# Attention in 64-row tiles, and 32-column tiles for the other products, in a fused gated mix of an S4D convolution and segmented attention

## The chip, the cores and the metric

The kernel runs on one core of a Trainium2 chip. The metric is device time in microseconds for one execution. The core has five engines that run on their own and wait for each other by semaphores: PE (matrix products into PSUM), DVE (vector), ACT (scalar functions), POOL (GpSimd) and SP, which issues most of the transfers. PE loads a block of weights and then streams columns past it. The array can be used whole (128 rows x 128 columns), or as tiles of 64 or 32 rows or columns; tiles on different rows or columns can work side by side.

## The reference

Input `x` is 2048 x 448. The result mixes two branches with a gate per row.

```python
x = A_u                                            # (1, 2048, 448)
g = sigmoid((x * gate_w).sum(-1, keepdims=True))
# A: diagonal state space model as a long convolution, N = 256 states
K = 2 * einsum("dn,dnl->dl", C, exp((A * dt)[:, :, None] * pos)).real
y = irfft(rfft(x.T, 2 * L) * rfft(K, 2 * L))[..., :L].T + x * D_skip
# B: 16 heads of 28, four segments of 512, softmax attention and a running memory
for s in range(4):
    p = softmax(qs @ ks.T * scale + mask)           # causal within the segment
    a_dot = p @ vs
    a_mem = (phi(qs) @ M) / (phi(qs) @ z + 1e-6)
    o = g_h * a_mem + (1 - g_h) * a_dot
    M, z = M + phi(ks).T @ vs, z + phi(ks).sum()
b = concat(o) @ wo
return g * y + (1 - g) * b
```

All data is float32.

## The kernel before, in words

The program has two halves. The **first half** builds the convolution kernel `kb` from sines and exponentials, and beside it runs the projections to q, k and v, the memory terms and the first Fourier step of `x`. Tables of numbers (FEED, FILL, UNREAD, VECTOR) say at each slot how many steps of the projections are fed in, how many Fourier steps fill gaps, how many dummy matmuls go ahead of a sum (`turn_over`, UNREAD), and whether copies run on DVE or on ACT. q and k go to DRAM as a high and a low part (`QD`, `KD`), 32 rows per head: 28 of the head and one (row 28) of ones in k, which in q takes the negated maximum of each row.

The **second half** works on 16 units, each of one segment and four heads. Its order is a string of words, PROGRAM, each letter one step, recorded in this order on PE:

- `l` loads q and k of a unit (`load`), `A` computes one block of maxima (`maxima`): a product of q and k for two heads, then a reduction on DVE. After six `A` comes `B`, which transposes the maxima and writes them, high and low, into row 28 of q through a small transfer that POOL issues.
- `W` is one of six steps of `weigh`: for one block and two heads, products of k and q and an exponential on ACT. Three products (high x high, low x high, high x low) give the accuracy. `P` does two `W` of the same block abreast, with four heads on the four 32-row groups.
- `V` multiplies the weights `PT` with the values (four 32-column tiles), `E` is a step of a segment's end (division, memory, output projection `out_mm`), `K` a Fourier step of `kb` (`transform_k`), `C` a step of the convolution (`transform`, `product`, `back`), and `b`, `j`, `z` the last Fourier step (`finish`), `D` a division in the last segment.
- `t` is a filler, a product of a tile of ones (`wz`) that nobody reads.

PSUM has two `ps_m` and three `ps_a` buffers; nearly all steps need a `ps_a` buffer, which ACT or DVE sets free. The loads go to SP's queue in the order in which a scheduler places them among the other transfers; a load waits there until its buffer is free. There are four buffers each for q and k.

A float32 product runs as two passes over its columns, each with its own weight load; q, k and the split parts are of a kind that takes one pass.

## Time and profile before

| | us |
|---|---|
| median of three runs | 835.19 (832.37 to 835.3) |
| the profiled execution | 836.45 |
| its span, first to last instruction | 834.7 |
| PE busy | 727.2 (87%) |
| DVE busy | 569.5 (68%) |
| ACT busy | 555.2 (67%) |
| POOL busy | 239.1 (29%) |

Busy time is the union of an engine's instructions, so it is no rate: matmuls are pipelined, and each one's row also holds the time that it takes to come out of the array. Where the prediction needs the time that a group holds PE, it takes the distance from the group's first start to the next group's first start. In a row, `ps_a<-qu,ku` names the tile written and the tiles read, `32*128` the rows and columns of the array that are used, and `x6` the number of instructions. The first product of the second half (`kb` with `s1k`) starts at 437.8 us.

### The profile page before, as it was taken

What the parts mean: (1) busy time and instruction counts of PE and PEld (TensorE: products, weight loads), DVE (VectorE), ACT (ScalarE), POOL (GpSimd) and SP (SyncE); (2) the same over time, 40 slices, a digit from 0 to 9 for tenths busy, and PEclk for the clock granted to TensorE, in tenths of its full rate; (3) what the DMA queues carried; (4) which work ended last, traced back from release to release, by engine and by line L of the source; (5) the groups of instructions that cost most, each with busy time, mean ns of one, the idle gap of its engine ahead of it and who ended that gap; (6) DMA issues with size and microseconds to landing.
All of it is one profiled execution on the core that took longest, in us unless ns stands there. A gap on an engine that the chain in (4) does not pass through costs nothing.

```text
span 834.7 us, 19015 instructions
## 1 busy us (share of the span) xinstructions
PE 727.2 (87%) x7557; PEld 398.3 (48%) x7582; DVE 569.5 (68%) x1134; ACT 555.2 (67%) x663; POOL 239.1 (29%) x249
## 2 busy tenths in 40 slices
PE   1576998999879999799979899999999899988977
PEld 1353555665546655456644454444444344444433
DVE  7969489857989579886785864544554545666773
ACT  3767789979999899988872266765466544641320
POOL 4404210111001111011110035564545545752210
PEclk9879999999999999999995889999999899999999
DMA  8527775145552455513647877685466565556775
GB/s 206 157 60 241 226 241 175 59 137 181 176 169 66 137 177 178 170 54 135 201 150 295 306 238 219 196 269 172 171 215 215 156 233 175 194 185 253 216 227 150
DMA packets 91987, 153.99 MB, mean 184 GB/s; under 512 B 23106, under 2 KB 60346, under 8 KB 91850
## 3 DMA queue, kind: packets, MB, share of 16 engines
q1 hardware_dynamic: 82826, 141.70, 53.2%
q10 hardware_dynamic: 7424, 9.18, 3.2%
q0 software_dynamic: 1648, 1.89, 0.8%
q8 instruction: 60, 0.98, 0.5%
q14 instruction: 29, 0.24, 0.1%
HBM read 91.74 MB, written 60.63 MB: 183 GB/s over the span
## 4 chain that ended last, share of the span: by engine, by line
PE 45%; DVE 18%; ACT 16%; DMA 9%; issue 7%; POOL 2%; SPq 1%; ACTq 0%; DVEq 0%; POOLq 0%
PE ps_m L1429 19%; PE ps_a L1429 18%; ACT cs L1394 7%; DVE Y L399 4%; DVE jk L1063 4%; PE ps_arg L1429 3%; PE ps_k L1429 3%; DVE X L395 2%; DVE Y L400 2%; ACT L1394 2%; PE ps_m L1432 1%; DMA r<-RD 1%; ACT EX L1394 1%; DMA bt<-BB 1%; DMA ce<-in_c_ce 1%
## 5 line engine op out<-in xcount | busy, mean ns | idle before, releaser
L1063 DVE CUSTOM_DVE_ANT_0 jk<-ps_a,mk 128x512 f32<-128x512 f32 (+3 forms) x256 | 125.1, 489 | 77.7 <-PE ps_a L1429 69.6
L361 POOL TENSOR_TENSOR EX<-EX,cab 128x1024 f32<-128x1024 f32 x28 | 53.5, 1913 | 301.7 <-ACT EX L1394 277.5
L1099 ACT ACTIVATE PT<-ps_a 128x1024 f32<-128x1024 f32 (+1 forms) x96 | 83.0, 880 | 69.6 <-PE ps_a L1429 68.6
L1394 ACT ACTIVATE cs<-ps_arg 128x1024 f32<-128x1024 f32 x111 | 107.4, 1023 | 1.4 <-DVE Y L400 0.8
L1429 PE MATMUL ps_a<-qu,ku 32*128 32x384 f32 (+3 forms) x768 | 78.3, 351 | 5.9 <-DVE mx L1063 5.0
L1429 PE MATMUL ps_m<-xh,w 128*128 128x512 f32 x224 | 81.8, 417 | 1.7 <-DMA w<-WD 1.4
L395 DVE TENSOR_TENSOR X<-EX,cs 128x1024 f32<-128x1024 f32 x56 | 69.2, 1236 | 17.8 <-ACT cs L1394 17.6
L663 POOL TENSOR_TENSOR pr<-us,ks 128x896 f32<-128x896 f32 x32 | 67.1, 2095 | 30.2 <-ACT us L662 30.1
L1110 POOL TENSOR_SCALAR_AFFINE_SELECT PT<-PT 128x256 f32<-128x256 f32 (+1 forms) x96 | 48.2, 507 | 93.3 <-ACT PT L1099 91.7
L1429 PE MATMUL ps_k<-Y,X 128*32 128x64 f32 x3584 | 62.2, 221 | 14.3 <-DVE Y L400 14.0
L1429 PEld LDWEIGHTS ps_k<-Y,X 128*32 128x32 f32 x3584 | 52.9, 110 | 39.1 <-DVE Y L400 27.0
L399 DVE TENSOR_TENSOR Y<-EY,cs 128x1024 f32<-128x1024 f32 x56 | 70.0, 1251 | 0.0
L1429 PEld LDWEIGHTS ps_a<-qu,ku 32*128 32x128 f32 x768 | 55.3, 193 | 20.2 <-DVE mx L1063 9.7
L1394 ACT ACTIVATE EY<-ps_arg 128x1024 f32<-128x1024 f32 x52 | 53.0, 1034 | 17.8 <-PE ps_arg L1429 16.4
L1394 ACT ACTIVATE cs<-cs 128x1024 f32<-128x1024 f32 x56 | 59.3, 1059 | 1.8
L401 DVE SCALAR_TENSOR_TENSOR Y<-EY,cs 128x512 f32<-128x512 f32 x56 | 40.9, 732 | 27.9 <-ACT cs L1394 25.8
L1429 PEld LDWEIGHTS ps_m<-xh,w 128*128 128x128 f32 x224 | 42.0, 187 | 21.9 <-issue 7.9
L1429 PE MATMUL ps_a<-ku,qu 32*128 32x512 f32 (+3 forms) x256 | 47.4, 404 | 4.5 <-DVE mx L1063 1.7
L1429 PE MATMUL ps_arg<-ct,lh 64*128 64x512 bf16 x224 | 45.5, 380 | 6.0 <-ACT cs L1394 4.3
L1429 PE MATMUL ps_m<-xl,w 128*128 128x512 f32 x128 | 50.2, 393 | 0.0
L1429 PEld LDWEIGHTS <-lh 64*128 64x128 bf16 x392 | 22.9, 95 | 55.2 <-issue 41.7
L1429 PEld LDWEIGHTS ps_a<-ku,qu 32*128 32x128 f32 x256 | 23.1, 195 | 48.2 <-issue 21.8
(215 smaller groups left out, 1429.4 us busy)
## 6 DMA issues: line engine op xcount, KB each, us to landing
w<-WD SPq DMA_DIRECT2D x32, 448.0 KB, 4.5
qu<-QD SPq DMA_DIRECT2D x16, 512.0 KB, 4.0
ku<-KD SPq DMA_DIRECT2D x16, 512.0 KB, 5.1
GU<-gs SPq DMA_DIRECT2D x32, 224.0 KB, 2.4
GK<-gs SPq DMA_DIRECT2D x8, 896.0 KB, 4.7
gk<-GK SPq DMA_DIRECT2D x32, 224.0 KB, 3.8
gu<-GU SPq DMA_DIRECT2D x32, 224.0 KB, 2.5
BB<-bs ACTq DMA_DIRECT2D x16, 448.0 KB, 4.5
```

Of the source, the lines that this page charges most:

```text
L361: nc.gpsimd.tensor_tensor(o, o, cab, ALU.mult)
L395: v.tensor_tensor(X, ex, t[:, :, 0], ALU.mult)
L399: v.tensor_tensor(Y[:, :, :, :32], lo, y[:, :, :, ::-1], ALU.mult)
L400: v.tensor_tensor(Y[:, 0, :, 32:], ey[:, :, 32:], y[:, 0], ALU.mult)
L401: v.scalar_tensor_tensor(Y[:, 1, :, 32:], ey[:, :, 32:], -1.0, y[:, 1], ALU.mult, ALU.mult)
L663: nc.gpsimd.tensor_tensor(pr[c], us, ks.pop(c), ALU.mult)
L1063: v.tensor_tensor_reduce(junk[:, :n], pt[:, x, o : o + n], k.mk[:, SEG - n :], 1.0, -3e38, ALU.add, ALU.max, mx[:, 3 - t, h : h + 1],)
L1099: nc.scalar.activation(PT[:, 2 * hp : 2 * hp + 2, 512 * b : 512 * b + n], pt[:, :, :n], AF.Exp, scale=SCALE)
L1110: nc.gpsimd.affine_select(sl, sl, pat, ALU.is_ge, 0.0, base=0, channel_multiplier=-1)
L1394: x = op(*args, **kw)
L1429: tc.keep_in_program_order(nc.tensor.matmul(*args, **kw))
L1432: tc.keep_in_program_order(nc.tensor.transpose(*args))
```

## The change

- **Attention in tiles of 64 rows.** q of a head stands with its high part on 32 rows and its low part on the next 32; two heads on 64 rows each fill the array, and the other two heads of the unit stand behind them in the tile. k stands twice, once for each part, as a high and a low tile. One product over 64 rows now adds q's high and low part times k's high part; a second one does the same with k's low part. So `weigh` takes two products where it took three, and `maxima` still one. The two heads of a step use the rows 0 to 63 and 64 to 127; which pair it is no longer decides on the rows. The words for two steps abreast (`P`) are gone.
- **Loads.** A unit's load is eight transfers of 32 rows (four of q, four of k) instead of two; unit 0 is loaded by POOL's queue. The negated maxima go out in four transfers instead of one. There are three buffers each for q and k instead of four; the first two `PT` tiles and the first tile of values get their place ahead of them.
- **Tiles of 32 columns.** `mm4` cuts a product into four of 32 columns of weights side by side: back transform, last Fourier step, output projection, division, and the filler `t`. A new filler `T` is a pair of products in 64-row tiles. `k` is a `K` whose copies both run on ACT.
- **Tables and words.** FEED, FILL, UNREAD, VECTOR and PROGRAM are written anew. In the first half the gate's weights come by POOL's queue, and the second copy of 64 columns of `xin` is made by POOL from the first instead of by a transfer.

```diff
@@ out_mm; back, last, divide alike
-            k.mm(
+            k.mm4(
...
@@ load
-        for t, T, src in (("q", Q, k.QD), ("k", K, k.KD)):
-            T[i] = ap.tile([128, 2, SEG], F32R, tag=t, name=t + "u", bufs=4)
-            x = k.dma(T[i].bitcast(F32), src[s, hg])
-        if i < 3:
+        Q[i] = ap.tile([128, 2, SEG], F32R, tag="q", name="qu", bufs=3)
+        K[i] = ap.tile([128, 2, 2, SEG], F32R, tag="k", name="ku", bufs=3)
+        qd = k.QD[s, hg].rearrange("(p j e) b q -> j b e p q", p=2, j=2)
+        kd = k.KD[s, hg].rearrange("(p j e) b q -> j e p b q", p=2, j=2)
+        for j in range(2):
+            for b in range(2):
+                r = slice(64 * j + 32 * b, 64 * j + 32 * b + 32)
+                queue = k.dma if i else k.pdma
+                queue(Q[i][r].bitcast(F32), qd[j, b])
+                x = queue(K[i][r].bitcast(F32), kd[j])
+        if 0 < i < 3:
@@ maxima
-                    h = 2 * hp + x
-                    r = slice(32 * h, 32 * h + 32)
+                    r = slice(64 * x, 64 * x + 64)
                     k.mm(
-                        pt[:, x, o : o + n], q[r, 0, 128 * qt : 128 * qt + 128], kk[r, 0, :n],
-                        start=True, stop=True, tile_position=(32 * h, 0),
+                        pt[:, x, o : o + n], q[r, hp, 128 * qt : 128 * qt + 128], kk[r, hp, 0, :n],
+                        start=True, stop=True, tile_position=(64 * x, 0),
                     )
...
-        k.pdma(q.rearrange("(j e) i q -> e j i q", e=32)[28].bitcast(F32), mn.bitcast(F32))
+        for b in range(2):
+            for j in range(2):
+                r = 64 * j + 32 * b + 28
+                k.pdma(q[r : r + 1].bitcast(F32), mn[2 * j : 2 * j + 2, b].bitcast(F32))
@@ weigh
-                for a, (x, y) in enumerate(((0, 0), (1, 0), (0, 1))):
-                    for (_, hp), pt in zip(now, pts):
-                        for z in range(2):
-                            h = 2 * hp + z
-                            r = slice(32 * h, 32 * h + 32)
-                            k.mm(
-                                pt[:, z, o : o + n], kk[r, x, 128 * kt : 128 * kt + 128], q[r, y, 128 * kt :],
-                                start=(a == 0), stop=(a == 2), tile_position=(32 * h, 0),
-                            )
+                for a in range(2):
+                    for z in range(2):
+                        r = slice(64 * z, 64 * z + 64)
+                        k.mm(
+                            pt[:, z, o : o + n], kk[r, hp, a, 128 * kt : 128 * kt + 128], q[r, hp, 128 * kt :],
+                            start=(a == 0), stop=(a == 1), tile_position=(64 * z, 0),
+                        )
@@ turn_over
-            k.mm(pt, wz[:, :128], wz, start=True, stop=True)
+            k.mm4(pt, wz[:, :128], wz, start=True, stop=True)
+    def turn_halves(n):
+        pt = k.ps("a")
+        for _ in range(n):
+            for h in range(2):
+                r = slice(64 * h, 64 * h + 64)
+                k.mm(pt[:, h], wz[r, :128], wz[r], start=True, stop=True, tile_position=(64 * h, 0))
...
@@ gated_mix
+    def mm4(out, w, x, **kw):
+        first = kw.pop("first", 0)
+        for j in range(0, w.shape[-1], 32):
+            mm(out[j : j + 32], w[:, j : j + 32], x, tile_position=(0, first + j), **kw)
@@ PROGRAM, one row of it
-ECAPVBCAWCtAWCtttAWCCtttAWCWV
+WCCVWVBCAWtECCtAWEEEtttCAWAtttttAWWVttttCAl
```

The tables' other rows tell a reader nothing by themselves; the order in which PE's instructions stand says more. Here are places in the two built programs, where a row reads line, operation, tile written and tiles read, shape and count. In the middle of the second half, PE before (`ku,qu` is a maxima pair, `qu,ku` a weigh step, `wo,pvs` the output projection, `gk,cf` a transform of the convolution):

```order
L1429 MATMUL ps_a<-ku,qu 128x256 x2
L1429 MATMUL ps_a<-qu,ku 128x256 x6
L1429 MATMUL ps_m<-wo,pvs 128x448 x4
L1429 MATMUL ps_a<-gk,cf 128x448 x2
L1429 MATMUL ps_a<-ku,qu 128x512 x2
L1429 MATMUL ps_a<-qu,ku 128x512 x6
```

and PE after, in a stretch of the same stage (`gu,cf` is the other transform, `r_7650,sel` a step of the division):

```order
L1453 MATMUL ps_a<-qu,ku 128x512 x4
L1453 MATMUL ps_a<-gu,cf 128x448 x2
L1453 MATMUL ps_m<-r_7650,sel 128x512
L1453 MATMUL ps_a<-ku,qu 128x256 x2
L1453 MATMUL ps_a<-gk,cf 128x448 x2
L1453 MATMUL ps_a<-ku,qu 128x256 x2
```

A weigh step has four products for two heads where it had six, and the maxima stand beside transforms, which now have the same tile shape, as often as beside a weigh step. At the start of the second half, PE before:

```order
L1429 MATMUL ps_k<-Y,X 32x64 x32
L1429 MATMUL ps_a<-kb,s1k 128x448 x8
L1429 MATMUL ps_a<-ku,qu 128x512 x2
L1429 MATMUL ps_a<-kb,s1k 128x448 x8
L1429 MATMUL ps_a<-ku,qu 128x512 x2
```

and PE after:

```order
L1453 MATMUL ps_k<-Y,X 32x64 x32
L1453 MATMUL ps_a<-kb,s1k 128x448 x16
L1453 MATMUL ps_a<-ku,qu 128x512 x2
L1453 MATMUL ps_a<-kb,s1k 128x448 x8
L1453 MATMUL ps_a<-ku,qu 128x512 x2
```

Two steps of `K` now stand ahead of the first maxima instead of one. The load of unit 0 stands on POOL behind the last scaling of the first half (`EX`), where it was on SP behind the last stores of the first half; the loads of units 1 and 2 stay on SP.

106 lines of the change are left out of this document (58 added, 48 removed), and 64 rows, old and new, of tables (FEED, FILL, UNREAD, VECTOR).

## The prediction

> **What bounds the kernel now.** I cut the execution into stages first: the end of the first half (the first matmul on `kb`, 437.8 us), the first product of weights and values (488.9), and the twelfth (729.3). The view of busy time by stretches gives, after the two times, PE, weight loads, DVE, ACT, POOL, the granted clock, the DMA share and GB/s.
>
> ```profile
> 0.00:437.80 437.80, 363.50 (x5102) 228.73 (x5106) 346.47 (x484) 368.28 (x435) 82.97 (x65) 0.96 0.50 157
> 437.80:488.90 51.10, 46.18 (x253) 24.18 (x256) 33.15 (x105) 13.21 (x16) 3.86 (x8) 0.68 0.83 306
> 488.90:729.30 240.40, 228.83 (x1632) 104.26 (x1645) 124.98 (x419) 144.73 (x175) 125.00 (x138) 0.98 0.63 198
> 729.30:834.70 105.40, 88.70 (x575) 41.12 (x577) 64.93 (x130) 28.98 (x38) 27.23 (x40) 0.96 0.66 208
> ```
>
> The middle stage (240.4 us) is bound by PE: 228.8 us busy at a clock of 0.98, while ACT has 144.7, DVE 125.0 and POOL 125.0. The opening of the second half (51.1 us) has PE busy for 46.2 us, but at a clock of 0.68 and with the DMA engines at 0.83. The tail (105.4) is a mixture of PE and waits. In the first half ACT, PE and DVE all stand near 80%.
>
> Then I read the order of matmuls in the middle for what PE does with that time; each row is start, duration, line, and the tile's rows*columns.
>
> ```profile
> 504.69 0.49 PE L1429 MATMUL ps_a<-ku,qu 32*128 32x512 f32 x2
> 504.80 0.96 PE L1429 MATMUL ps_a<-qu,ku 32*128 32x512 f32 x6
> 505.70 0.39 PE L1429 MATMUL ps_m<-wz 128*128 128x512 bf16 x1
> ...
> 529.42 1.02 PE L1429 MATMUL ps_a<-gu,cf 64*128 64x448 f32 x4
> 530.28 0.92 PE L1429 MATMUL ps_a<-gk,cf 64*128 64x448 f32 x4
> 531.13 0.50 PE L1429 MATMUL ps_a<-ku,qu 32*128 32x384 f32 x4
> 531.52 1.07 PE L1429 MATMUL ps_a<-qu,ku 32*128 32x384 f32 x12
> 532.53 1.02 PE L1429 MATMUL ps_a<-gu,cf 64*128 64x448 f32 x4
> ...
> 537.13 0.39 PE L1429 MATMUL ps_a<-ku,qu 32*128 32x256 f32 x2
> 537.14 0.62 PE L1429 MATMUL ps_a<-qu,ku 32*128 32x256 f32 x6
> 537.68 1.02 PE L1429 MATMUL ps_a<-gk,cf 64*128 64x448 f32 x4
> 538.64 0.82 PE L1429 MATMUL ps_m<-wz 128*128 128x512 bf16 x3
> 539.39 0.38 PE L1429 MATMUL ps_a<-ku,qu 32*128 32x256 f32 x2
> ```
>
> Three things are to be seen. First, **a change of tile shape costs time at both ends**. The group at 537.68 (shape entered and left by a change) holds PE until 538.64, 0.96 us. The one at 529.42 (entered by a change, followed by its own shape) takes 0.86, and the one at 530.28 (entered from its own shape, left by a change) 0.85. So the work itself is 0.86+0.85-0.96 = 0.75 us, entering costs 0.11 and leaving 0.10: 0.2 us for a visit. Second, **a maxima pair runs beside the first product of a weigh step**: 504.69 and 504.80, 537.13 and 537.14. They stand on different 32-row groups, so four tiles work at once. Third, three fillers take 0.75 us (538.64 to 539.39) with one change in it: about 0.22 us each for 512 columns.
>
> **The change part by part.** Sums are made against the profiled execution (836.45 us, span 834.7); the median of the runs shown is 835.19, 1.3 us lower.
>
> *Three products to two.* Now a step of maxima and weigh takes 1.01 us for the first block (504.69 to 505.70), 1.40 for the second (531.13 to 532.53) and 0.55 for the third (537.13 to 537.68): 2.96 us for one head pair, 16 x 2 = 32 of them. After it, maxima and weigh use the same two 64-row tiles, so nothing runs beside anything: three slots in a row (one maxima, two weigh). A slot of 512 columns is taken at the filler's 0.22 us, 384 columns at 0.17, and 128 or 256 columns at 0.12, since a weight load, which took 0.11 where it stood open at the entry, does not get shorter. First block: 0.11 + 3 x 0.22 + 0.10 = 0.87; second: 0.11 + 3 x (0.17 + 0.12) + 0.10 = 1.08; third: 0.11 + 3 x 0.12 + 0.10 = 0.57. Sum 2.52, or 0.44 less; 32 times that is 14 us, some 10 us of it in the middle stage (11 of 16 units). I note how little that is: the third product goes, but so does the four-tile overlap that hid the maxima. The nine double steps (the word P, two weigh steps abreast in three slots) now need four slots: 0.22 us each, five of them in the middle, 1 us back.
>
> *Fewer shapes.* Weigh, maxima and both transforms of the convolution are now all 64*128; values, back transform, output projection and fillers all 128*32. Counted in the built order of the second half without fillers, the changes of shape fall from 201 to 143. With the fillers they are 280 in both, because there are more fillers, and in the middle stage 209 against 184: 25 fewer x 0.2 = 5 us. A product cut into four column tiles streams the same columns side by side, so I cost the cutting itself at nothing. What supports this is the product of weights and values, which already runs so; two rows of the order in time, then two groups with their busy time and mean ns.
>
> ```profile
> 509.52 2.36 PE L1429 MATMUL ps_m<-PT,V 128*32 128x512 f32 x32
> 511.82 0.60 PE L1432 MATMUL ps_m<-ident,mx 128*4 128x128 f32 x4
> L1429 PE MATMUL ps_m<-wo,pvs 128*128 128x448 f32 x96 | 40.6, 569 | 1.0 <-DVE pvs L1187 0.7 <-PE ps_m L1429 0.3
> L1429 PE MATMUL ps_m<-wz 128*128 128x512 bf16 x119 | 37.6, 399 | 5.4 <-ACT tb L1203 1.7 <-DVE pvs L1187 1.5 <-issue 1.2
> ```
>
> Four heads of 512+384+256+128 = 1280 columns took 2.30 us, 1.8 ns per column of four tiles. The output projection holds 40.6 us in 96 records of half a product, which is 0.42 us for 448 columns, or 1.9 ns per column for its two halves. The two are equal, so the bounds of this edit are -2 and +2 us.
>
> [...]
>
> *More fillers.* The words hold 196 `t` and 17 `T` for 141 `t`: 72 more x 0.22 = 16 us if none lay in a wait. By place: 45 more before the first values product, where PE waits anyway, 9 more each in the middle and in the tail: 2 us each.
>
> *Loads and the maxima rows.* K now comes twice, 1 MB for 0.5 per unit, 8 MB in all, and a unit's load is eight issues instead of two; the maxima rows go by four POOL issues instead of one.
>
> ```profile
> 488.78 0.33 SPq L1445 DMA_DIRECT2D qu<-QD x1
> 489.15 0.43 SPq L1445 DMA_DIRECT2D ku<-KD x1
> qu<-QD SPq DMA_DIRECT2D x16, 512.0 KB, 4.0
> ku<-KD SPq DMA_DIRECT2D x16, 512.0 KB, 5.1
> L1075 POOL DMA_DIRECT2D qu<-mn x16 | 9.6, 602 | 56.0 <-DVE mn L1074 54.5 <-DVE mx L1063 1.5
> ```
>
> The SP issues go from 0.8 us to 4 x (0.33 + 0.43) = 3.0 us a unit, the POOL ones from 0.6 to 2.4. On SP the loads of the convolution stand behind them, on POOL the masks of `PT` and the products `pr`. POOL has 115 us idle in the middle, against 11 x 1.8 = 20 us added, and a unit's rows are issued three or more weigh steps ahead of their first use. I take nothing, with +8 us as the upper bound (a third rival has the case where it fails).
>
> *The opening.* Here the first load is late; two rows of the chain of waits, two of POOL, and the busy time of the first 20 us:
>
> ```profile
> 436.97 5.04 DMA ku<-KD
> 442.15 3.39 PE ps_a L1429 x16
> 411.64 1.91 POOL L361 TENSOR_TENSOR EX<-EX,cab 128x1024 f32<-128x1024 f32 x1 [20.70 <-ACT EX L1394]
> 415.54 1.91 POOL L361 TENSOR_TENSOR EX<-EX,cab 128x1024 f32<-128x1024 f32 x1 [1.99 <-ACT EX L1394]
> 440.00:460.00 20.00, 17.68 (x90) 9.42 (x83) 11.89 (x32) 4.58 (x5) 0.00 (x0) 0.57 0.78 300
> ```
>
> After the change unit 0 is loaded on POOL, behind its last scaling (over at 417.5), so it can be there before 437; that takes the 5 us wait off the chain. But the K transforms that follow ran at half clock (0.57 here), 3.39 us for sixteen matmuls, and go on until the clock comes back. I count some 66 fillers in this stage, 66 x 0.22 = 15 us of PE, put where PE waits. The work done by the same mark is more (nine weigh steps instead of seven). Between -8 (wait gone, clock up) and +6 (1.5 MB more at 306 GB/s is 5 us, where the DMA share is already 0.83) I take 0.
>
> *First half.* The new tables hold the same sum of steps (249) and move three copies net from ACT to DVE; 70 more dummy matmuls at 0.07 us each make at most 5 us of PE.
>
> ```profile
> 428.82 1.07 PE L1429 MATMUL ps_k<-ct,one 128*128 128x128 bf16 x16
> ```
>
> The sixteen small loads that go are replaced by sixteen POOL copies behind the large ones. I take 0, between -5 and +5.
>
> **Sum.** Middle: -10 (products) +1 (P) -5 (shapes) +2 (fillers) = -12. Tail: four units' share of the products -3.5, P +1, fillers +2, six more changes of shape +1: 0. Opening 0, first half 0. 836.45 - 12 = 824.5, and less the 1.3: about 823; I say 824.
>
> **The rivals.**
>
> 1. *The opening too gets shorter.* If the clock is up from 437 on, the K transforms halve. Half clock costs the opening 51.1 x (1-0.68) = 16 us of PE at most, of which I allow 10, and the 5 us wait goes: 824 - 14 = 810. For it: the first load moves to an idle queue. Against: the words again begin with two K transforms, and the DMA share is 0.83.
>
> 2. *Nothing is won.* The freed slots are taken by fillers and new waits: DVE's reductions and the three `ps_a` buffers set the pace, as DVE waits for `ps_a` and PE for DVE in turn. Then the middle stays at 240: 835. For it: as many changes of shape as before, and 72 more fillers. Against: DVE and ACT are at 52 and 60% in the middle.
>
> 3. *Loads come late (slower).* There are three buffers instead of four, and in the words the load of unit 8, for one, stands six words ahead of that unit's first maxima (load, W, V, B, C, E, A): 0.7 + 2.3 + 0.6 + 0.95 us by the rows above and about 1 for E, some 5.8 us of PE, where before a dozen words and more lay between. Landing then takes 5.1 us plus the 2.2 us that the last issue is later. If SP does not run ahead of PE, PE stands about 1.5 us at each of 13 units, 20 us: 844. It decides from 0.9 us per unit on, where 12 us are used up. Against: SP's issues wait only for buffers, and the third buffer is free one to four weigh steps earlier.
>
> 4. *Loads of weights on the same row group stand open.* All 384 slots of attention are now on the same two groups. If no load could pass under a matmul on its own group, the 288 slots that I counted as covered would take 0.11 us and then their columns (0.22, 0.16, 0.05, 0.11) instead of 0.22, 0.17, 0.12, 0.12: 0.085 us more on average, 24 us in all, so 848. Against it are the rows above: the step at 504.69 took 1.01 us with three weigh products on one group; with each load open it would be 0.11 + 3 x (0.11 + 0.22) + 0.10 = 1.20. [...]
>
> **How the numbers follow.** Forecast 0.50; rival 1 0.20, rival 2 0.16, rival 3 0.10, rival 4 0.04. A measurement of this kernel tells about 0.5% (4 us) from no change. The forecast's own range is 815 to 832, nearly all of it faster; with rival 1 and a tenth of rival 2 that makes 0.71 faster. Same: most of rival 2 and a little of the forecast, 0.16. Slower: rivals 3 and 4, 0.13. For 8 in 10 the range must hold the forecast, most of rival 1 and rival 2: 805 to 838.
>
> **What would show it.** Right: the stretch between the first and the twelfth values product is near 228 us with PE over 95% busy; a step of the first block takes about 0.9 us and of the second 1.1; the maxima no longer start beside a weigh product; a transform followed by a weigh step shows no 0.1 us gap. Wrong: PE idle ended by loads of `ku` (rival 3), equal spacing of 0.33 us between weigh slots (rival 4), a middle stage as long as now with more fillers in it (rival 2). Rival 1 shows as a clock near 1 in the first 20 us of the second half. A first half that moves by more than 5 us would make the sum wrong whatever attention does.

## The result, and the profile after

The changed kernel takes 871.64 us (median of 4 runs, 869.44 to 877.92), beside 834.07 us for the kernel before on the same chip: a ratio of 1.046, 95% interval 1.0405 to 1.0523. It is slower by 4.6%, where 1.3% faster was forecast. Some executions of one and the same kernel took over 1.5% longer than its fastest (836.73 us beside 823.21 in `b_first_p0`); they count in the medians below and not in the ratios, which are each taken against the kernel before on the same chip. The profiled execution took 877.92 us with a span of 876.2. Cut at the same marks (first matmul on `kb`, first and twelfth product of weights and values), the view of busy time by stretches gives for the changed kernel, columns as in the prediction:

```profile
0.00:431.40 431.40, 369.60 (x5174) 234.32 (x5174) 350.57 (x487) 367.20 (x432) 93.73 (x92) 0.97 0.52 162
431.40:493.70 62.30, 56.34 (x495) 25.48 (x495) 32.45 (x106) 15.72 (x19) 7.46 (x15) 0.86 0.80 245
493.70:762.70 269.00, 240.84 (x2062) 109.30 (x2060) 127.48 (x409) 139.82 (x173) 139.32 (x169) 0.93 0.74 198
762.70:876.20 113.50, 97.62 (x946) 40.12 (x944) 64.77 (x134) 29.41 (x39) 31.64 (x50) 0.92 0.71 208
```

Against 437.8, 51.1, 240.4 and 105.4 us before: the first half is 6 us shorter, the opening 11 us longer, the middle 29 us longer and the tail 8 us longer. In the middle PE is busy for 12 us more and waits for 17 us more (269.0 - 240.84 against 240.4 - 228.83).

What it waits for stands in the page's groups and DMA issues and in the first row of the waits view (us in total, times, longest):

```profile
L1453 PE MATMUL ps_a<-ku,qu 64*128 64x512 f32 (+3 forms) x256 | 54.1, 433 | 26.1 <-DMA ku<-KD 16.9
L1453 PE MATMUL ps_a<-qu,ku 64*128 64x256 f32 (+3 forms) x512 | 68.7, 370 | 7.8 <-DVE mx L1077 4.3
...
ku<-KD SPq DMA_DIRECT2D x60, 256.0 KB, 5.5
...
gk<-GK SPq DMA_DIRECT2D x32, 224.0 KB, 5.4
gu<-GU SPq DMA_DIRECT2D x32, 224.0 KB, 6.9
PE ps_a L1453 <- DMA ku<-KD: 16.9, 8, 3.7
```

and, for the two loads of spectra, on the page of the kernel before:

```profile
gk<-GK SPq DMA_DIRECT2D x32, 224.0 KB, 3.8
gu<-GU SPq DMA_DIRECT2D x32, 224.0 KB, 2.5
```

The first maxima of a unit now stand still for the unit's own keys; and the spectra `gk` and `gu`, whose loads stand behind the units' loads on SP, land 5.4 and 6.9 us after their issue, where the kernel before had 3.8 and 2.5. The chain of waits, cut to the middle stage, says the same in shares of that stage:

```profile
by line: PE ps_a L1453 30.6%; PE ps_m L1453 19.6%; DMA ku<-KD 13.9%; SPq L1479 5.8%; DMA xt<-in_A_u 5.0%; DVE jk L1077 4.0%; issue 3.2%; DMA TB<-xt 3.0%; DVE xt L1226 2.3%; DMA dn<-pvs 2.3%; POOL pr L663 1.6%; POOL qu L1092 1.3%; POOL xt L1
```

13.9% of 268 us is 37 us in which the chain runs through a load of `ku`, and 16 us more (5.8%) through SP's issues. One unit in order of time, SP's queue and then PE:

```profile
535.71 0.32 SPq L1479 DMA_DIRECT2D qu<-QD  x1
536.08 0.70 SPq L1479 DMA_DIRECT2D ku<-KD  x1
...
539.27 0.43 SPq L1479 DMA_DIRECT2D ku<-KD  x1
539.80 0.37 SPq L1479 DMA_DIRECT2D gk<-GK  x1
```

```profile
535.17 1.71 PE L1453 MATMUL ps_a<-qu,ku 64*128 64x256 f32 x12
...
543.18 0.54 PE L1453 MATMUL ps_a<-ku,qu 64*128 64x512 f32 x1
545.91 0.47 PE L1453 MATMUL ps_a<-ku,qu 64*128 64x512 f32 x1 [2.20 <-DMA ku<-KD]
```

The load of unit 5 needs the buffer of unit 2. Unit 2's last weigh step is among the twelve matmuls from 535.17, the first of the eight issues comes at 535.71, the last at 539.27, and the chain gives that one 6.50 us to land. The first matmul of unit 5's maxima is at 543.18, and the second stands 2.20 us for the last piece. In the kernel before, every unit's load but that of unit 0 was issued 15 us or more ahead of its first maxima: unit 4's at 488.78 and 489.15, its first maxima at 504.69 (rows in the prediction).

### The profile page after: what moved, and what is told of

The parts are those of the page before. It is cut to its first block, busy times and chain, and to the rows that moved or that the text cites. A ratio compares the mean times of both kernels' runs of the same rounds, so it can differ in the third digit from the quotient of the medians.

```text
span 876.2 us, 21521 instructions
## 1 busy us (share of the span) xinstructions
PE 764.4 (87%) x8673; PEld 409.2 (47%) x8673; DVE 575.3 (66%) x1136; ACT 552.2 (63%) x661; POOL 272.2 (31%) x324
## 4 chain that ended last, share of the span: by engine, by line
PE 42%; DMA 16%; DVE 14%; ACT 11%; issue 9%; SPq 5%; POOL 2%; ACTq 0%; DVEq 0%; POOLq 0%
PE ps_m L1453 20%; PE ps_a L1453 12%; DMA ku<-KD 6%; PE ps_arg L1453 4%; ACT cs L1418 4%; PE ps_k L1453 4%; SPq L1479 3%; DVE Y L399 3%; DVE X L395 2%; DVE jk L1077 2%; DVE Y L400 2%; PE ps_m L1456 2%; DMA xt<-in_A_u 2%; DMA WD<-wsp 1%; ACT L1418 1%
## 5 line engine op out<-in xcount | busy, mean ns | idle before, releaser
L395 DVE TENSOR_TENSOR X<-EX,cs 128x1024 f32<-128x1024 f32 x56 | 70.2, 1254 | 13.9 <-ACT cs L1418 13.8
L1453 PE MATMUL ps_a<-ku,qu 64*128 64x512 f32 (+3 forms) x256 | 54.1, 433 | 26.1 <-DMA ku<-KD 16.9
L1453 PE MATMUL ps_a<-qu,ku 64*128 64x256 f32 (+3 forms) x512 | 68.7, 370 | 7.8 <-DVE mx L1077 4.3
L1453 PE MATMUL ps_m<-wz 128*32 128x512 bf16 x784 | 66.0, 415 | 0.2
L1453 PEld LDWEIGHTS ps_a<-qu,ku 64*128 64x128 f32 x512 | 46.8, 200 | 33.2 <-issue 13.4
L401 DVE SCALAR_TENSOR_TENSOR Y<-EY,cs 128x512 f32<-128x512 f32 x56 | 42.7, 764 | 26.6 <-ACT cs L1418 24.0
L1453 PEld LDWEIGHTS ps_a<-ku,qu 64*128 64x128 f32 x256 | 25.2, 198 | 63.6 <-issue 41.2
L1453 PEld LDWEIGHTS ps_m<-xh,w 128*128 128x128 f32 x224 | 42.0, 187 | 21.3 <-issue 9.0
L1092 POOL DMA_DIRECT2D qu<-mn x64 | 32.6, 515 | 58.6 <-ACT mn L1087 57.9
L1088 DVE SCALAR_TENSOR_TENSOR mn<-ps_m,mn 4x512 fp32r<-4x512 f32 x16 | 10.8, 678 | 60.4 <-ACT mn L1087 60.2
```

Of the source, the lines that this page charges most:

```text
L395: v.tensor_tensor(X, ex, t[:, :, 0], ALU.mult)
L401: v.scalar_tensor_tensor(Y[:, 1, :, 32:], ey[:, :, 32:], -1.0, y[:, 1], ALU.mult, ALU.mult)
L1092: k.pdma(q[r : r + 1].bitcast(F32), mn[2 * j : 2 * j + 2, b].bitcast(F32))
L1453: tc.keep_in_program_order(nc.tensor.matmul(*args, **kw))
```

## The loads

**Without the loads.** The first question is what all late loading costs together. This kernel leaves out the loads of units 3 to 15 (13 x 1.5 MB); these units compute on the tiles of units 0 to 2, so its output is of other data.

```diff
     def load(i):
         if i >= 16:
             return
+        if i >= 3:
+            Q[i], K[i] = first3[i % 3]
+            return
...
+        first3[i] = Q[i], K[i]
```

> The changed kernel in which units 3 to 15 load no q and k: they work on the tiles of units 0 to 2 again (13 of 16 loads left out, so the output is of other data). Theory 1 (late loads: with three buffers a load can be issued only when the weigh steps of the unit three before are over, and that unit's first maxima is then 5 to 10 us away): the waits on ku go, 872 falls to 835 to 848. Theory 2 (the 72 added fillers and their changes of shape hold PE): 862 to 872, since the fillers are all still there. Theory 3 (cutting products into 32-column tiles costs PE time): 862 to 872.

Measured 835.01 us (828.87 to 837.92), ratio 0.998 [0.994, 1.002]: 37 us less than the changed kernel, and just the time of the kernel before. Its middle stage and its tail in the view by stretches:

```profile
491.80:733.40 241.60, 230.77 (x2062) 104.89 (x2060) 128.19 (x409) 139.82 (x173) 139.61 (x169) 0.96 0.49 149
733.40:833.50 100.10, 88.68 (x946) 37.38 (x944) 65.07 (x134) 29.21 (x39) 32.12 (x50) 1.00 0.66 209
```

So 27 of the middle's 29 us belong to the loads (269.0 against 241.6), and 13 of the tail (113.5 against 100.1), more than it had grown. It also says that what is left of the change, with its loads free, wins nothing as a whole.

This trace also shows how much time a load has, since nothing stands for loads in it. From the last weigh step of the unit three before, which frees the buffer, to a unit's first maxima it has 6.9 to 19.5 us, with a median of 10.4. The eight issues and the landing of the last piece took 3.6 + 6.5, some 10 us, in the rows above, so the units with 7 to 9 us come too late. In the kernel before, with four buffers, the same distance (from the unit four before) is 16.0 to 33.3 us. Waits of PE that end with a load of `ku` add up to 16.9 us only; how the rest of the 37 us divides between the loads queued behind and the doubled bytes was not separated.

**A buffer less, alone.** The kernel before with three `q` and `k` buffers and nothing else changed:

```diff
-            T[i] = ap.tile([128, 2, SEG], F32R, tag=t, name=t + "u", bufs=4)
+            T[i] = ap.tile([128, 2, SEG], F32R, tag=t, name=t + "u", bufs=3)
```

> The kernel before with three buffers for q and k instead of four; nothing else is changed. Theory 1: the same words with the same 32-row products lose as the changed kernel with these words did: 900 to 960. If the loss belongs to the doubled k and the eight issues: 835 to 845.

Measured 917.45 us, ratio 1.102 [1.094, 1.110]: 82 us for the fourth buffer. In its waits view:

```profile
PE ps_a L1429 <- DMA ku<-KD: 60.4, 14, 7.5
```

A unit is seven `W` (six weigh steps and the masks). Counted in these words, each `l` from unit 3 on stands four to six `W` ahead of the sixth of the unit three before. With four buffers that costs nothing that shows (827.19 us with the loads of units 3 to 15 and 826.17 without them, both behind the new first half, below); with three, a load has to wait until that unit is through, and the chain of waits from 490 to 790 us runs for 62 us (20.7%) through loads of `ku`. How late the transfers behind it on SP's queue come was not shown.

**The old words with the new loads.** The changed kernel with the words of the kernel before, each `P` written as `WW`:

```diff
 PROGRAM = """
-KKlAkAtttltAAtAtKAttKKKttttttttttttVTTTTTKAttBttAttGtTTTCTAAtttA
...
-tCttWWVBCCAWtAtAWttVCWtAWtAtWCCtAClw
...
+KlAKAAlKAKKAAtAKKBAKtVGCttAtttAtttAttt
...
+lAVWWtCABCAWCtAWCtttWACWtttACWwAV
...
```

> The changed kernel with the words of the kernel before (each P written as WW). The loads stand about a unit earlier in these words, but there are still three buffers. Theory 1: a load placed early holds SP's queue until its buffer is free, and what stands behind it is late too: 865 to 890. Theory 4 (the new words are the fault, not the buffers): 830 to 850.

Measured 971.25 us, ratio 1.163 [1.154, 1.171], far above both theories. So the new words are not what makes the loads late. They soften it: each of their `l` stands one or two `W` behind the sixth of the unit whose buffer it takes. The loads' price is 147 us under the old words (971.25 against 824.63 without them, a kernel further below) and 37 under the new ones (871.64 against 835.01). In the trace of the old words without loads the time from release to first maxima has a median of 1.3 us, where the new words left 10.4.

**The fourth buffer given back.** Queries and the high part of the keys get four buffers, and the low part has tiles of its own (three, loaded later by a word `m`, since only the weigh steps read them). To make room, `ks` has 2 buffers for 3, `bs` 1 for 2, `bt` 4 for 5. Old words.

```diff
-        Q[i] = ap.tile([128, 2, SEG], F32R, tag="q", name="qu", bufs=3)
-        K[i] = ap.tile([128, 2, 2, SEG], F32R, tag="k", name="ku", bufs=3)
+        Q[i] = ap.tile([128, 2, SEG], F32R, tag="q", name="qu", bufs=4)
+        K[i] = [ap.tile([128, 2, SEG], F32R, tag="k", name="ku", bufs=4), None]
...
+        K[i][1] = ap.tile([128, 2, SEG], F32R, tag="kl", name="kl", bufs=3)
```

> The changed kernel with k's high and low part in tiles of their own: four buffers for q and k high (loaded together), three for k low, which is loaded later by a step of its own. Room for it comes from ks (3 to 2), bs (2 to 1) and bt (5 to 4). The words are those of the kernel before, P written as WW. With three buffers these words took 971 us. Theory 1 (the missing fourth buffer is the cause of the loss): the loads are issued a unit ahead again, no waits on ku, 815 to 835. If it is the eight issues or the 8 MB more: 850 or more.

Measured 862.22 us, ratio 1.034 [1.026, 1.042]. The buffers, with the later load of the low part, are worth 109 us under these words (971 to 862). Together with the 82 us of the run before, the missing buffer is the cause of most of the loss under the old words. But 28 us above the kernel before remain, where theory 1 had none: this is the outcome that was set down for the eight issues or the 8 MB more. The remainder is not pure, since a unit's load is now twelve issues and ScalarE waits 17.8 us at its copies into `ks`, which has one buffer less; its parts were not separated.

**Eight issues, alone.** The kernel before with each load cut into four of 32 rows; same bytes, buffers and words.

```diff
-            x = k.dma(T[i].bitcast(F32), src[s, hg])
+            for r in range(0, 128, 32):
+                x = k.dma(T[i][r : r + 32].bitcast(F32), src[s, hg, r : r + 32])
```

> The kernel before with each of a unit's two loads cut into four of 32 rows, so eight issues on SP as in the changed kernel, with the same bytes, buffers and words. Theory 10a (the number of issues alone delays nothing, since the loads are issued 15 to 30 us ahead): 832 to 838. Theory 10b (eight issues fill SP's queue so that the convolution's loads behind them come late): 845 or more.

Measured 841.67 us (840.77 to 844.03), ratio 1.011 [1.006, 1.015]: 8 us, between the two theories. In its one profile the opening is 2.3 us and the middle 3.2 us longer than before. The same ten microseconds of the opening, while the units 0 to 2 are loaded, of the kernel before and then of this one:

```profile
450.00:460.00 10.00, 9.25 (x50) 4.76 (x45) 5.61 (x18) 2.75 (x3) 0.00 (x0) 0.63 0.77 310
```

```profile
450.00:460.00 10.00, 9.68 (x54) 4.69 (x50) 6.47 (x22) 2.40 (x3) 0.00 (x0) 0.66 1.04 305
```

The rate is the same (310 and 305 GB/s), but the DMA engines are busy for 0.77 of the time in the one and for all of it in the other: with the loads in pieces of 32 rows, the traffic of this stretch occupies them a third longer per byte (403 against 293 GB/s per full share). Why the pieces occupy the engines longer was not shown: no run here separates their 32 rows from their smaller size, or the 8 us from the time of six more issues a unit.

## The two products and the words

**Two products against three, loads out of the way.** Two kernels with the same words (the old ones) and the same new first half, both without the loads of units 3 to 15: one with the new tiles and two products, one with the old tiles and three. Both compute on other data, as above. The first is the kernel without loads above with the old words put in as before; in the second the same lines go into `load` of the kernel with the new first half (shown near the end):

```diff
     def load(i):
...
+        if i >= 3:
+            Q[i], K[i] = first3[i % 3]
+            return
         for t, T, src in (("q", Q, k.QD), ("k", K, k.KD)):
...
```

> The changed kernel without the loads of units 3 to 15 (those units reuse the tiles of units 0 to 2, so the output is of other data), and with the words of the kernel before, each double step replaced by two single ones. Since no load can hold the queue here, it shows the new tiles and two products under the old order. Changes of tile shape fall from 280 to 237 in the second half. Theory 8a (the new words lose what two products save, because they split attention's visits and add 45 fillers in the opening): the middle stage falls from the 241.6 us of the same kernel under the new words to 225 to 232, and the time from 835 to 815 to 825. Theory 8b (two products save nothing whatever the order is, since the stage is set by VectorE's and ScalarE's steps and the tiles of PSUM): the middle stage stays at 236 to 243 and the time at 828 to 838.

> The kernel before with the change's first half, and with the loads of units 3 to 15 left out (those units reuse the tiles of units 0 to 2, so the output is of other data): the counterpart, with 32-row tiles and three products, of the changed kernel without loads under the old words (824.63 us, middle stage 233.5). Theory 8a' (two products are worth some 6 us of the middle stage, 239.8 to 233.5): without loads the old tiles keep a middle stage of 238 to 241, and the time is 823 to 828. Theory 8c (the difference was the loads' and not the products'): the middle stage falls to 231 to 235 with three products too, and the time to 816 to 821, so that the new tiles bring nothing at all.

Measured 824.63 us (821.10 to 828.27), ratio 0.990 [0.985, 0.995], and 826.17 us (821.85 to 829.66), ratio 0.992 [0.989, 0.995]. The opening and the middle of each by stretches, new tiles first:

```profile
431.10:486.30 55.20, 42.83 (x303) 20.82 (x303) 33.06 (x106) 13.31 (x16) 6.78 (x14) 0.81 0.85 268
486.30:719.80 233.50, 222.35 (x2032) 99.60 (x2030) 124.14 (x417) 143.34 (x175) 141.73 (x170) 1.00 0.50 153
```

```profile
431.50:476.30 44.80, 39.70 (x253) 20.10 (x256) 33.05 (x104) 13.19 (x16) 3.85 (x8) 0.85 0.88 329
476.30:715.80 239.50, 228.99 (x1636) 104.62 (x1653) 125.00 (x420) 144.51 (x175) 124.91 (x138) 0.98 0.49 149
```

The middle is 6.0 us shorter with two products (8a', not 8c; of the first pair of theories the middle falls between 8a and 8b, the time in 8a), and the opening 10 us longer. The times are 1.5 us apart, which is within the noise: given free late loads and the better words, the new tiles win nothing that can be told, though they win 6 us in the middle. The two kernels also differ in the rest of the second half (the cutting into 32 columns, `P` as `WW`, the maxima rows in four transfers, the doubled keys of units 0 to 2).

**Where the 6 us come from.** It does not look like the product. A step pair of the first block (maxima and weigh of one head pair), in the order of time, of the kernel before and of the new tiles under the old words:

```profile
508.62 0.50 PE L1429 MATMUL ps_a<-ku,qu 32*128 32x512 f32 x2
508.63 0.96 PE L1429 MATMUL ps_a<-qu,ku 32*128 32x512 f32 x6
509.52 1.07 PE L1429 MATMUL ps_m<-PT,V 128*32 128x512 f32 x8
...
512.34 1.02 PE L1429 MATMUL ps_a<-gk,cf 64*128 64x448 f32 x4
513.30 0.44 PE L1429 MATMUL ps_a<-ku,qu 32*128 32x384 f32 x2
...
514.38 0.65 PE L1429 MATMUL ps_a<-gu,cf 64*128 64x448 f32 x2
```

```profile
505.17 0.50 PE L1457 MATMUL ps_a<-ku,qu 64*128 64x512 f32 x2
505.50 0.63 PE L1457 MATMUL ps_a<-qu,ku 64*128 64x512 f32 x4
506.06 0.64 PE L1457 MATMUL ps_m<-PT,V 128*32 128x512 f32 x4
...
513.49 0.50 PE L1457 MATMUL ps_a<-ku,qu 64*128 64x384 f32 x4
513.83 0.74 PE L1457 MATMUL ps_a<-qu,ku 64*128 64x384 f32 x8
514.50 0.62 PE L1457 MATMUL ps_m<-wz 128*32 128x512 bf16 x8
...
582.32 1.02 PE L1457 MATMUL ps_a<-gu,cf 64*128 64x448 f32 x4
582.83 0.75 PE L1457 MATMUL ps_a<-ku,qu 64*128 64x512 f32 x2
583.40 0.63 PE L1457 MATMUL ps_a<-qu,ku 64*128 64x512 f32 x4
583.97 0.64 PE L1457 MATMUL ps_m<-PT,V 128*32 128x512 f32 x4
```

First block: 509.52 - 508.62 = 0.90 us with three products, 506.06 - 505.17 = 0.89 with two. Second block: 1.08 and 1.01. Over the middle stage of the kernel before, the pair's medians are 0.96, 1.09 and 0.55 us (14, 16 and 16 pairs; seven of the 14 take 0.90 or 0.91). The single starts say why: before, the maxima start at 508.62 and the three weigh products at 508.63, 508.97 and 509.20; after, the maxima at 505.17 and the two weigh products at 505.50 and 505.73. Both have three places in time. The maxima ran beside the first weigh product on free row groups; now they take the place of the product that went. What is won is the change of shape, as far as the rows tell. Behind a transform of the same shape the maxima start at once (582.32 to 582.83 is 0.51 us for the transform, where it held PE 0.96 with a change at both ends, 512.34 to 513.30), but take 0.57 us to their successor instead of 0.33: transform and pair together 1.65 us, against 0.96 + 0.89 = 1.85 with changes all round. That is 0.20 us, the price the prediction read. Nineteen transforms under the old words hold PE 0.51 us in this way (median), where before it was 0.95.

The price does not multiply out, though. Counted in the traces, with transposes as a shape of their own, the changes in the middle fall from 235 to 174 under the old words and to 193 under the new ones. (The 235 are from the kernel with the new first half alone, whose trace has a record of every filler in this stage.) The 61 would be 12 us at 0.2 each, and the stage got 6 us shorter. No run changes the shapes and nothing else. The nearest, with the cutting alone (`b_first_mm4`, below), has 22 changes fewer in its second half, and none of the 4 us that they would be worth shows in its time.

The holding time of each kind of work in the middle stage (from the start of each PE record to the start of the next, summed; us):

| kernel | attention + transforms | fillers | back transform | rest | sum |
|---|---|---|---|---|---|
| first half new, three products, no loads | 132.1 | 21.3 | 23.4 | 63.0 | 239.9 |
| first half new, three products, with loads | 128.5 | 24.3 | 23.2 | 63.8 | 239.8 |
| two products, old words, no loads | 121.6 | 25.9 | 22.5 | 63.7 | 233.5 |
| two products, new words, no loads | 118.6 | 30.2 | 28.8 | 63.5 | 241.2 |
| changed kernel | 139.2 | 34.0 | 29.4 | 66.4 | 269.0 |

The first two rows have the same words in the second half, but the trace of the first has records of only 72 of the 87 fillers in this stage; the time of the other 15 counts there with the group ahead of them. So the second row is the one to compare with. Old words: -6.9 us on attention and transforms, +1.6 for fillers. New words: 3 us less again on attention and transforms, but +4.3 on fillers and +6.3 on the back transform, of which 4.9 are waits; the gain is spent. The time says the same: 824.63 us with the old words, 835.01 with the new, so without late loads the new words cost 10 us.

**Fillers.** The changed kernel without the 140 of its 213 `t` and `T` that stand behind the first values product (nobody reads what they compute):

```diff
-tCttWWVBCCAWtAtAWttVCWtAWtAtWCCtAClw
+tCttWWVBCCAWAAWVCWAWAWCCAClw
...
```

> The changed kernel without any filler (t and T) after the first product of weights and values; all loads are there. Theory 1: the fillers lie in waits for loads, so the time stays at 866 to 876, or rises if the clock falls. Theory 2: the fillers hold PE by 0.22 us each and two changes of shape by 0.2 us each run, so 840 to 855.

Measured 862.33 us, ratio 1.033 [1.026, 1.040]: 9 us less than the changed kernel, outside the range of both theories. And the same words without the loads:

> The changed kernel without the loads of units 3 to 15 (they work on the tiles of units 0 to 2) and without fillers after the first values product. The run without these loads took 835 us: the waits on ku are worth 36 us, but the 12 us that the middle stage was to gain are not there. Theory 2b (the fillers stand between products that now have one shape, so each run of fillers costs two changes of shape beside its own time): the middle stage falls from 241.6 to about 215 to 225 us, the whole to 812 to 822. Theory 5 (DVE, ACT and three PSUM buffers set the pace, and the fillers lie in their waits): the middle stage stays at 236 to 242, the whole at 828 to 838.

Measured 827.07 us (823.62 to 831.61), ratio 0.991 [0.987, 0.994]: 8 us less than with fillers, next to the range of theory 5 and far from 2b. Its middle and the largest waits of PE in it:

```profile
490.30:727.00 236.70, 207.87 (x1678) 98.51 (x1676) 128.05 (x409) 139.94 (x174) 140.14 (x169) 0.94 0.50 152
PE ps_a L1457 <- DVE mx L1081: 14.7, 18, 5.2
PE ps_a L1457 <- ACT PT L1116: 5.5, 11, 0.8
PE ps_a L1457 <- ACT us L662: 4.2, 10, 0.8
```

PE is busy for 23 us less (230.77 to 207.87), the stage is only 4.9 shorter: of the 30.2 us of fillers most lay in front of these waits for the readers of `ps_a`, VectorE's reductions first (14.7, 5.5 and 4.2 us here; 9.6, 0.2 and 0.3 with the fillers). The granted clock fell by little (0.94 for 0.96). This bears out the second rival in part: the middle ends at 234 to 237 us whether PE is busy for 222 us of it (old words) or for 208 (no fillers).

**Cutting into 32 columns.** The changed kernel with all products whole again:

```diff
     def mm4(out, w, x, **kw):
-        first = kw.pop("first", 0)
-        for j in range(0, w.shape[-1], 32):
-            mm(out[j : j + 32], w[:, j : j + 32], x, tile_position=(0, first + j), **kw)
+        first = kw.pop("first", None)
+        if first is not None:
+            kw["tile_position"] = (0, first)
+        mm(out, w, x, **kw)
```

> The changed kernel with the other products of the second half and the filler t whole again instead of in four 32-column tiles; attention stays in 64-row tiles. Theory 1: within 5 us of 872. Theory 3: 850 to 862, as the output projection, the back transform and 196 fillers get cheaper.

Measured 871.16 us, ratio 1.044 [1.036, 1.051], against 871.64 with the cutting: nothing that can be told. And the other way round, the kernel before with the new first half and the cutting alone:

```diff
-            k.mm(pt, wz[:, :128], wz, start=True, stop=True)
+            k.mm4(pt, wz[:, :128], wz, start=True, stop=True)
...
-            k.mm(
+            k.mm4(
                 po, pvss[s][:, hg, 128 * t : 128 * t + 128], wo[:, hg],
...
```

> The kernel before with the change's first half and with the cutting into tiles of 32 columns (back transform, output projection, normalizing, fillers), attention left in 32-row tiles with three products. Changes of tile shape in the second half fall from 280 to 258, at 0.2 us each 4 us. Theory 9a (a change of shape costs what the rows said wherever it stands): 4 us below the kernel with the first half alone. Theory 9b (cutting is worth nothing, as it was when it was undone in the changed kernel, because those changes of shape lie in waits): within 2 us of the kernel with the first half alone.

Measured 829.57 us (820.96 to 835.17), ratio 0.991 [0.988, 0.995], against 827.19 and 0.992 without the cutting: nothing that can be told (9b).

## The opening

The opening took 62.3 us instead of 51.1, although the wait for unit 0's load is gone. The first suspect was ScalarE's copy into `gs`, which has one buffer less and waited 5.18 us in the opening for the store before it. The changed kernel with four `gs`:

```diff
-        gs = fp.tile([128, 4, 4, 112], F32, tag="gs", name="gs", bufs=3)
+        gs = fp.tile([128, 4, 4, 112], F32, tag="gs", name="gs", bufs=4)
```

> The changed kernel with four buffers for the K transforms' copies (gs) instead of three. In its trace a copy waited 5 us for a store of GK to land, and the opening took 62 us for 51. Theory 6 (the fewer gs buffers lengthen the opening): opening 57 us or less, the whole 864 to 868. Otherwise (the words, with 47 more fillers and nine weigh steps, and the slower rows of maxima): 61 to 63 and 870 to 874.

Measured 868.57 us, ratio 1.042 [1.034, 1.050], with an opening of 61.1 us: not the cause.

The second suspect is the DMA engines. Under the old words without later loads the opening was 55.2 us with 1.5 MB each for units 0 to 2 (row above); this kernel also leaves out the load of unit 2 (all later units compute on the tiles of units 0 and 1):

```diff
-        if i >= 3:
-            Q[i], K[i] = first3[i % 3]
+        if i >= 2:
+            Q[i], K[i] = first3[i % 2]
```

> The changed kernel under the old words with the loads of units 2 to 15 left out (they reuse the tiles of units 0 and 1; output of other data): 1.5 MB and eight issues less in the opening than the same kernel that loads three units, whose opening took 55.2 us with the DMA engines fully busy from 442 to 458 us at 258 to 283 GB/s. Theory 11a (the opening is longer because the loads in pieces of 32 rows and the second copy of K fill the DMA engines): the opening falls to 46 to 50 us and the time to 816 to 821. Theory 11b (it is longer because of the maxima rows in four POOL issues or because of the tiles): the opening stays at 53 to 56.

Measured 818.29 us (816.87 to 822.90), ratio 0.984 [0.980, 0.987], 6 us less.

```profile
427.20:475.80 48.60, 38.96 (x307) 19.05 (x309) 33.39 (x107) 13.57 (x16) 7.40 (x15) 0.94 0.80 272
475.80:711.50 235.70, 225.27 (x2035) 100.04 (x2035) 123.50 (x415) 142.76 (x174) 140.85 (x169) 0.99 0.50 152
```

The opening falls by 6.6 us and the middle grows by 2.2: unit 2's load of 1.5 MB, as much as the doubled keys add over units 0 to 2, is worth that much in the opening (11a). What it holds up is not shown; the stores and loads of the K transforms go beside it. In the kernel that loads it, the ten microseconds from 440 have the DMA engines at full share for 258 GB/s; the kernel with the old tiles, all loads and the same first half (`b_first`, in the next section) has 343 GB/s there at 0.87:

```profile
440.00:450.00 10.00, 7.05 (x50) 3.38 (x50) 5.46 (x19) 1.85 (x3) 0.00 (x0) 1.00 1.04 258
```

```profile
440.00:450.00 10.00, 9.57 (x51) 4.59 (x47) 6.55 (x20) 2.75 (x3) 0.00 (x0) 0.66 0.87 343
```

So some 7 us are the loads' bytes and their pieces, as far as the load of unit 2 stands for them. The new words add 7 more under the same loads (62.2 us against 55.2, both without the later loads). Together that is more than the 11 us, because the old tiles' opening is itself 2 to 6 us shorter after the new first half (49.4 and 44.8). What part of the words' 7 us is fillers and what is the order of K transforms and maxima was not separated.

## A version that beats both

**The first half alone.** The kernel before with the four tables, the gate weights on POOL's queue and the copy of `xin` on POOL; second half untouched.

```diff
-    2, 0, 3, 0, 1, 0, 2, 0, 1, 3, 8, 0, 0,
+    2, 0, 3, 0, 1, 0, 3, 0, 0, 3, 8, 0, 0,
...
-    nc.sync.dma_start(gw[:, :3, 0], k.gate_w[:384].rearrange("(k p) -> p k", p=128))
+    k.pdma(gw[:, :3, 0], k.gate_w[:384].rearrange("(k p) -> p k", p=128))
...
-                nc.sync.dma_start(xin[:, D:], k.u[rs, 384:])
+            nc.gpsimd.tensor_copy(xin[:, D:], xin[:, 384:D])
```

> The kernel before with the change's first half alone: its four tables, the gate weights on POOL's queue, the second columns of xin copied on POOL. The second half stays as it was. Theory 7a (the first half is simply shorter and the second half follows it): the first half ends at 428 to 432 us as in every kernel that has the new tables, the opening keeps its 51 us, and the time is 825 to 829. Theory 7b (the start of the second half hangs on something with its own time, such as what still has to be stored, so that an earlier start is waited away): the first half ends 6 us earlier and the opening takes 57 us or more, as in the changed kernel, and the time is 833 to 836.

Measured 827.19 us (824.59 to 837.76, 10 runs), ratio 0.992 [0.989, 0.995].

```profile
0.00:429.00 429.00, 370.42 (x5174) 234.91 (x5175) 350.06 (x487) 367.12 (x432) 89.86 (x84) 0.95 0.51 159
429.00:478.40 49.40, 45.01 (x260) 22.86 (x262) 33.55 (x106) 13.45 (x16) 3.89 (x8) 0.74 0.85 320
478.40:718.20 239.80, 230.48 (x1647) 103.53 (x1645) 124.68 (x417) 144.38 (x175) 124.96 (x137) 0.99 0.62 198
```

The first half is 9 us shorter in this profile (437.8 to 429.0), the middle is as before: 7a. This kernel beats the kernel before by 0.8% and the changed one by 5%. Which of its edits gives the gain was not separated. Beside it, the kernel without later loads (826.17) says that in the old arrangement the loads cost nothing that can be told.

**And unit 0 on POOL's queue**, as in the changed kernel:

```diff
-            x = k.dma(T[i].bitcast(F32), src[s, hg])
+            x = (k.dma if i else k.pdma)(T[i].bitcast(F32), src[s, hg])
```

> The kernel before with the change's first half and with unit 0 loaded on POOL's queue, so that its load does not stand behind SP's stores: a candidate to beat both. In the kernel with the first half alone the chain has 4.66 us of waiting for ku from 428.18. Theory 12a (that wait goes and the rest follows): 822 to 825. Theory 12b (the K transforms' half clock or the next loads end last there anyway): 826 to 829.

Measured 828.91 us (823.21 to 836.73, 12 runs), ratio 0.995 [0.992, 0.998]. Its one profile has an opening of 45.4 us, 4 less than without the edit, but the times show no gain (12b).

## Why the prediction was wrong

The account, from kernel to kernel by their medians: 834 before; 827 with the new first half; 826 with the later loads free; 825 with the new tiles, two products and cutting under the old words; 835 with the new words; 872 with the loads back. Forecast were -12 us; measured -7, -1, -1.5, +10 and +37. The medians are from several chips, and the steps of -1 and -1.5 are within the noise.

*Loads and the maxima rows* is the step that decided the sign. "I take nothing, with +8 us as the upper bound" measured +37. The mechanism is the third rival's, given 0.10 and priced at 844: loads close ahead of the first maxima. The sentence against it drew the wrong conclusion: "SP's issues wait only for buffers, and the third buffer is free one to four weigh steps earlier". The buffer is indeed free one or two `W` ahead of each `l`, but its release is what the issue waits for, and behind the release come 3.6 us until the last issue (535.71 to 539.27) and 6.50 of landing, where the words leave 6.9 to 19.5 us. That rival's price of 1.5 us per unit, 20 us in all, came out on the right side partly by luck. Its terms add up to 5.6 us and not 5.8, and in the trace without loads 13.9 us lie between the release and the first maxima of its example, unit 8, since a step of `E` there takes over 3 us and not 1; other units are the short ones. The price took 5.1 us for landing from the kernel before, and counted neither the slower landing of pieces nor the loads of `gk` and `gu` behind them, which took 1.6 and 4.4 us longer. The upper bound of +8 was the length of work on SP and POOL, and left out a buffer's lifetime; the time between each release and the first maxima behind it, against those 10 us, would have given the sign.

*Three products to two*, "-10", measured about 0 in the pairs themselves. The three rows from which the step pair was priced (1.01, 1.40 and 0.55 us) were not typical: medians are 0.96, 1.09 and 0.55, 2.60 us for a head pair, and the forecast for the new tiles was 2.52. That forecast was near (medians of 0.90, 1.01 and 0.55 where no transform stands ahead); the saving was not there. The median of each group in place of three single rows would have shown it. The prediction noted that the maxima lose their cover, and that alone uses up what the third product gives back.

*Fewer shapes*, "-5", finds its price again in single rows (0.20 us a change); the traces count more changes gone than its 25 (42 in the middle, 61 under the old words), but the 61 came with 6 us in the stage and not 12. *Cutting* at 0 within 2 us holds, by both runs.

*More fillers*, "+2" in the middle for nine more: fillers hold PE 4.3 us longer there than under the old words, and taking all of them out won 4.9 us in the middle and 8 to 9 in the whole time. By place the prediction's 45, 9 and 9 add up to 63 and not to its 72; the words have 52, 9 and 11. *The P words* were not tried by themselves.

*The opening*, 0 between -8 and +6, measured +11. The upper bound used 306 GB/s for 1.5 MB; the new pieces moved at 258 with the engines full, and the words' part was not foreseen. *First half*, 0 between -5 and +5, measured -6 and -9 in the two profiles shown and -7 in the time, the largest gain of the change; the net move of three copies and the lesser loads were priced at nothing. In the profiles of all kernels with the new first half it ends between 426.9 and 431.7 us, so one profile tells it to some 3 us.

The first rival (clock up in the first 20 us) came half true: the opening's clock rose from 0.68 to 0.86, and the opening was longer all the same. The fourth (weight loads open on the same row group) is refuted by 0.89 us for the pair where it asked for 1.2. The second (nothing won in the middle) is what remains when the loads are taken out: 241.6 us against 240.4. Of the signs set down for the forecast, pairs of 0.9 and 1.0 us and the missing gap behind a transform did come, in the kernels without late loads; the shorter middle did not.

## What to carry to other kernels

Price an edit that costs a buffer by that buffer's lifetime: the time from the release to the first use must hold the issues and the landing (3.6 + 6.5 us here, where the words left 6.9 to 19.5), and count the loads queued behind them, which landed later too (5.4 and 6.9 us after issue, where it was 3.8 and 2.5). Here the maxima ran on idle row groups beside another product (starts at 508.62 and 508.63) and took no place in time of their own (0.90 us for the pair, 0.89 with a product less), and the new tiles gave that up. So look for what runs beside a product, in medians over the group and not in one row. And when a change has parts in different stages, time the parts alone: here a side part of the change was the gain.

## What the runs showed of the hardware

In one stretch of 10 us (450 to 460), loads cut into pieces of 32 rows kept the DMA engines fully busy at 305 GB/s, where whole loads of 128 rows needed 0.77 of them for 310, and the cut alone cost 8 us (ratio 1.011). One buffer less for two tiles of 512 KB cost 82 us under words that ask for the load early. A change of tile shape on PE cost 0.20 us in both places where it was read; 61 changes fewer in a stage came with 6 us. In the rows read, the group behind a transform started 0.45 us earlier without a change (0.51 us after the transform's start, where it was 0.96) but held PE 0.24 us longer (0.57 for 0.33), so one group's time told little there, and the sum over both did. And one trace lacks records of matmuls, those of 15 of a stage's 87 fillers. Summed from start to start, their time counts with the group ahead: 3.6 us moved so to attention and transforms.
